# Strassen's scheme for the output product of a gated FFN, in groups of two pairs

## The chip, the cores and the metric

The kernel runs on one core of a Trainium2 chip. The metric is the device time of one execution in microseconds (us). TensorE is called PE, VectorE DVE, ScalarE ACT, GpSimd POOL; SP issues the DMAs. PEld is PE's loading of weights.

## The reference, cut to what matters

```python
x = attention(q, k, v)                     # 2304 tokens x 512, window of 128, sloped bias
x = gelu_like(x @ w_in) @ w_out            # first FFN, 512 -> 2048 -> 512
g = x @ w_gate                             # second FFN, 512 -> 1536, twice
silu = g * (1.0 / (1.0 + np.exp(-g)))
val = x @ w_val
return (silu * val @ w_out2).astype(np.float32)   # 1536 -> 512
```

Inputs come as float64 words for the weights; the result has to be close to float32.

## The kernel before, in words

**Precision.** PE's operands have the type fp32r, a float32 word of fewer fraction bits. To keep float32's accuracy every operand is split in two: a rounded upper part, written by ACT as a copy, and the rest, written by DVE as a difference. A product is three matmuls: upper by upper, upper by rest, rest by upper.

**Stages.** Attention is computed in blocks of tokens and lies between the matmuls of the first FFN, in an order that is written out by hand for its start (`PLAN`) and set by hooks after it. The first FFN leaves its result y, transposed, in a scratch tensor in HBM (`y_scratch`). The second FFN, about 517 to 935 us, works on three super-blocks of 768 tokens. Its hidden width of 1536 is taken in six *pairs* of two 128-wide chunks, so there are 18 pair steps, q = 0 to 17. The words "gate" and "value" (G, V) stand for the products with `w_gate` and `w_val`, "O" for that with `w_out2`.

**Gate and value by Strassen.** For a pair, G and V are each a 2 x 2 block product (halves of the 512 inputs with halves of the tokens, for two chunks), and are computed with the Winograd form of Strassen's scheme: seven products in place of eight, numbered 1 to 7 (`product`, L690). One product is six matmuls of 384 columns (two chunks of the contraction by three splits). Products 1, 6, 7, 4 accumulate in one PSUM bank, 2 in a second, 5 and 3 in a third (`gv_steps`, L704). ACT copies partial sums out (`keep_copy`), DVE adds them (`add`), and behind products 2, 3, 7 and 4 of V a quarter of the pair's hidden tile is finished (`gate`, L719): tanh on ACT, two DVE instructions, then the split into upper part (ACT) and rest (DVE, L729).

**The output product** is done directly (`o_part`, L757): for each of six 128-token tiles, six matmuls of 512 columns into one bank, and one DVE instruction that adds it to an accumulator of 128 x 512 in SBUF (ACT copies it for the first pair of a super-block). It runs one pair behind G and V; the program puts one tile into the next pair's products and five behind them. After the last pair of a super-block each accumulator is written to the result.

**Preparation.** The Strassen sums of the weights are made on the chip while the first FFN runs, and the rest early in the second: a unit is one half of one pair of one matrix (36 units: 6 pairs x G, V, O x 2). `fetch` (L238) loads it, `fraction` turns the 64-bit words into float32, four DVE sums (L271) make the combinations, `halves` splits them (ACT L229, DVE L230), and two DMAs store them in a scratch tensor. Units of O have no sums: one split of 512 columns. `advance` spreads these steps over the program by a rate per block (`PACE`, `PACE_LATE`). The combinations of y (seven pieces per super-block, `y_steps`, L638) are made on DVE and ACT, with seven splits and four differences of 768 columns.

**What sets the order.** Instructions are recorded in program order, and a scheduler then orders them on each engine by its own estimate; the queues run in that order. Each weight tile of the second FFN (`load_weights`, L675) has one buffer: its next load waits on SP until PE has done its last product.

```python
for pair in ((1, 5), (2, 6), (3,), (7,), (4,)):   # gv_steps
    for m in "GV":
        for i in pair:
            step(m, i)
            yield m, i
```

Of the kernel before, what the change touches and what calls it, by code (L numbers as in the profile page):

```python
# [26 lines left out]
PACE = {0: 1.4, 2: 2.0, 3: 2.2, 4: 2.3}  # L27

PAUSE = 77

PACE_LATE = 0.6
# [3 lines left out]
LATER = 2.5  # L35

SUPER = 6

O_ORDER = 3, 4, 5, 0, 1, 2

A_BLOCKS = (4, 2, 4, 4, 4)
# [40 lines left out]
def attention_two_ffn(ctx: ExitStack, tc: tile.TileContext, q, k, v, w_in, w_out, w_gate, w_val, w_out2, yscr, wscr, woscr, out):  # L82
# [9 lines left out]
    DM = out.shape[1]  # L92
# [25 lines left out]
    wpool = ctx.enter_context(tc.tile_pool(name="w", bufs=1, reuse_waits="tile"))  # L118
    cvp = ctx.enter_context(tc.tile_pool(name="cv", bufs=2))
# [107 lines left out]

    def halves(t, at, src):
        nc.scalar.activation(out=t[:, at, 0, :], in_=src, func=AF.Copy)  # L229
        nc.vector.tensor_tensor(out=t[:, at, 1, :], in0=src, in1=t[:, at, 0, :].bitcast(F32), op=ALU.subtract)  # L230
# [3 lines left out]

    def fetch(slot, unit):

        m, p, h = unit
        pool, tag = slot()  # L238
        if m == "O":
            raw = pool.tile([P, 512, 2], U32, tag=tag, name="raw")  # L240
            src = w_out2[(2 * p + h) * P : (2 * p + h + 1) * P, :].bitcast(U32)
            nc.sync.dma_start(out=raw.rearrange("p c w -> p (c w)"), in_=src)
            return raw
        raw = pool.tile([P, 2, 2, P, 2], U32, tag=tag, name="raw")
        w = w_gate if m == "G" else w_val
        for f in range(2):
            src = w[2 * p + f].bitcast(U32).rearrange("p (a b c) -> p a b c", a=2, b=2)[:, :, h, :]
            nc.sync.dma_start(out=raw[:, f].rearrange("p a c w -> p a (c w)"), in_=src)
        return raw.rearrange("p f a c w -> p (f a c) w")

    def prepare(slot, raw, fetch_next, unit):

        m, p, h = unit
        cs = cvp.tile([P, 8, P], F32, tag="cv", name="cs")
        yield from fraction(raw, cs)
        fetch_next()
        if m == "O":
            pool, tag = slot()
# [16 lines left out]
        at = wscr[p, "GV".index(m)]  # L275
        pool, tag = slot()
        wa = pool.tile([P, 4, 2, P], F32R, tag=tag, name="wa")
# [5 lines left out]
        wb = cvp.tile([P, 3, 2, P], F32R, tag="cv", name="wb")  # L283
# [317 lines left out]
    def y_part(j, f):  # L601
# [36 lines left out]
    def y_steps(s, tile_of):  # L638
# [3 lines left out]
        def quarter(i, j):  # L642
            t = yrp.tile([P, 2, HT], F32, tag="yr", name="yr")
# [31 lines left out]
    def load_weights(q, m, half):  # L675
        p = q % NP2
        if m == "O":
            t = wpool.tile([P, 2, 2, 512], F32R, tag="w11" if q < NS * NP2 - 1 else "w0", name="wo")
            nc.sync.dma_start(out=t.bitcast(F32).rearrange("p f r c -> p (f r c)"), in_=woscr[p])
        else:  # L680
            n = (4, 3)[half]
            t = wpool.tile([P, 2, n, 2, P], F32R, tag=f"w{7 + 2 * 'GV'.index(m) + half}", name="wg")
            at = wscr[p, "GV".index(m)]
            nc.sync.dma_start(
                out=t.bitcast(F32).rearrange("p h s r c -> p (h s r c)"),
                in_=at[:, :2048] if half == 0 else at[:, 2048:],
            )
        w2[q, m, half] = t

    def product(q, m, i, bank_, start):  # L690
        half, at = W_OF[i]
        w, y = w2[q, m, half], y2[q // NP2, i]
        for kk in range(2):
            for n, (a, b) in enumerate(((0, 0), (0, 1), (1, 0))):
# [3 lines left out]
                    rhs=y[:, b, kk, :],  # L698
# [5 lines left out]
    def gv_steps(q):  # L704

        banks, kept, c = {}, {}, {}
        p2[q] = [wpool.tile([P, 2, 2 * HT], F32R, tag=f"w{12 + 2 * (q % 2) + f}", name="p2") for f in range(2)]
# [10 lines left out]

        def gate(i):  # L719
            f, j = i  # L720
            g, v = c["G", i], c["V", i]
            at = slice(j * HT, (j + 1) * HT)
            th = pp.tile([P, HT], F32, tag="th2", name="th2", bufs=3)
# [340 lines left out]
```

## Time and profile before

| what | value |
|---|---|
| median of three runs | 938.6 us (938.53 to 939.38) |
| profiled execution | 937.2 us, of which the span from first to last instruction is 935.4 |
| PE busy, share of the span | 916.7 us, 98% |
| DVE, ACT, POOL busy | 649.0, 422.0, 123.6 us |
| granted TensorE clock, mean | 0.994 |
| HBM read and written | 142.6 and 38.8 MB |

The busy time of an engine is the time in which at least one of its instructions runs. The chain that ended last is followed back from the last instruction; where its pieces follow each other without a gap, the engine named in them sets the time.

### The profile page before, as it was taken

How to read it: one execution, taken by the hardware profiler on the slowest of the kernel's cores; microseconds unless marked ns; L12 is line 12 of the kernel's file. 1: busy time of each engine (PE TensorE's matmuls, PEld its weight loads, DVE VectorE, ACT ScalarE, POOL GpSimd, SP SyncE). 2: the span in 40 equal slices, each digit the busy share in tenths (PEclk: the TensorE clock that was granted, in tenths of full speed). 3: DMA queues.
4: the chain of work that ended last, by engine and by line, in shares of the span. 5: the costliest groups of instructions: out<-in, count | busy, mean ns of one | idle time of the engine just before them, and what ended most of it. 6: DMA issues, size and time to landing. Idle time of an engine off the chain costs nothing.

```text
span 935.4 us, 15014 instructions
## 1 busy us (share of the span) xinstructions
PE 916.7 (98%) x5464; PEld 788.6 (84%) x5464; DVE 649.0 (69%) x1558; ACT 422.0 (45%) x968; POOL 123.6 (13%) x221
## 2 busy tenths in 40 slices
PE   6899999999999999999999999999999999999998
PEld 4577898787778877788888999999999999999996
DVE  7898797756876668757696567577545577545555
ACT  5565565643654446534454453344343343342321
POOL 4744004512331023300000000000000000000000
PEclk9899999999999999999999999999999999999999
DMA  8953202425543355435579488667765666766641
GB/s 319 358 200 134 93 13 62 151 93 166 176 150 128 126 195 192 139 108 191 196 267 325 166 333 322 226 211 265 265 209 203 208 255 220 275 213 216 212 151 67
DMA packets 62473, 182.38 MB, mean 195 GB/s; under 512 B 6080, under 2 KB 28096, under 8 KB 55488
## 3 DMA queue, kind: packets, MB, share of 16 engines
q1 hardware_dynamic: 62400, 181.43, 55.1%
q8 instruction: 43, 0.70, 0.3%
q14 instruction: 30, 0.25, 0.1%
HBM read 142.61 MB, written 38.80 MB: 194 GB/s over the span
## 4 chain that ended last, share of the span: by engine, by line
PE 86%; DVE 6%; DMA 3%; ACT 2%; POOL 1%; issue 1%; SPq 0%; DVEq 0%; POOLq 0%; ACTq 0%
PE sx L695 16%; PE o L765 16%; PE sz L695 8%; PE hp L561 6%; PE y L561 6%; PE hp L563 6%; PE y L563 6%; PE hp L562 6%; PE y L562 6%; PE sy L695 4%; PE xb L514 2%; PE sb L361 2%; PE pt L453 1%; DMA y_scratch<-yt 1%; DVE wraw L194 1%; POOL prob L421 1%
## 5 line engine op out<-in xcount | busy, mean ns | idle before, releaser
L695 PE MATMUL sx<-ya,wg 128*128 128x384 f32 x864 | 172.6, 336 | 0.0
L765 PE MATMUL o<-wo,p 128*128 128x512 f32 x648 | 158.9, 391 | 0.0
L695 PEld LDWEIGHTS sx<-ya,wg 128*128 128x128 f32 x864 | 153.1, 188 | 5.5 <-issue 0.3
L765 PEld LDWEIGHTS o<-wo,p 128*128 128x128 f32 x648 | 120.8, 188 | 21.4
L561 PE MATMUL hp<-xh,wt 128*128 128x512 f32 (+1 forms) x320 | 121.0, 378 | 0.5 <-DVE th L584 0.4
L563 PE MATMUL hp<-xh,wt 128*128 128x512 f32 (+1 forms) x320 | 118.1, 370 | 0.0
L562 PE MATMUL hp<-xl,wt 128*128 128x512 f32 (+1 forms) x320 | 118.0, 369 | 0.0
L562 PE MATMUL y<-gl,wt 128*128 128x512 f32 (+1 forms) x320 | 116.8, 371 | 0.5 <-DVE gl L592 0.5
L563 PE MATMUL y<-gh,wt 128*128 128x512 f32 (+1 forms) x320 | 117.0, 371 | 0.0
L561 PE MATMUL y<-gh,wt 128*128 128x512 f32 (+1 forms) x320 | 111.2, 377 | 0.2 <-DVE stat L386 0.2
L421 POOL TENSOR_SCALAR prob<-prob,stat 128x128 f32<-128x128 f32 x144 | 68.9, 498 | 204.4 <-DVE sb L331 55.7
L695 PE MATMUL sz<-ya,wg 128*128 128x384 f32 x432 | 84.1, 335 | 0.0
L592 DVE TENSOR_TENSOR gl<-th,gh 128x512 fp32r<-128x512 f32 (+1 forms) x80 | 52.4, 659 | 44.7 <-ACT gh L590 44.3
L590 ACT ACTIVATE gh<-th 128x512 fp32r<-128x512 f32 (+1 forms) x80 | 46.7, 586 | 78.5 <-PE y L563 55.2
L774 DVE SCALAR_TENSOR_TENSOR acc<-o,acc 128x512 f32<-128x512 f32 x90 | 61.4, 688 | 25.1 <-PE o L765 23.9
L695 PEld LDWEIGHTS sz<-ya,wg 128*128 128x128 f32 x432 | 75.8, 188 | 0.2
L716 DVE TENSOR_TENSOR c<-sy,pc 128x384 f32<-128x384 f32 x36 | 20.1, 558 | 79.5 <-PE sy L695 75.3
L561 PEld LDWEIGHTS hp<-xh,wt 128*128 128x128 f32 x320 | 60.4, 189 | 13.6 <-issue 1.6
L402 ACT ACTIVATE prob<-prob,stat 128x128 f32<-128x128 f32 x144 | 56.2, 392 | 34.4 <-DVE stat L386 34.3
L563 PEld LDWEIGHTS y<-gh,wt 128*128 128x128 f32 x320 | 60.3, 188 | 11.2 <-issue 1.0
L562 PEld LDWEIGHTS y<-gl,wt 128*128 128x128 f32 x320 | 60.3, 189 | 10.9 <-DVE gl L592 0.9
L563 PEld LDWEIGHTS hp<-xh,wt 128*128 128x128 f32 x320 | 60.2, 188 | 10.6
(90 smaller groups left out, 1385.6 us busy)
## 6 DMA issues: line engine op xcount, KB each, us to landing
wg<-w_scratch SPq DMA_DIRECT2D x36, 1024.0 KB, 6.9
wg<-w_scratch SPq DMA_DIRECT2D x36, 768.0 KB, 5.2
wo<-wo_scratch SPq DMA_DIRECT2D x18, 1024.0 KB, 6.9
w_scratch<-wa SPq DMA_DIRECT2D x24, 512.0 KB, 2.7
w_scratch<-wb SPq DMA_DIRECT2D x24, 384.0 KB, 3.5
wraw<-in_moe_w_in SPq DMA_DIRECT2D x16, 512.0 KB, 6.7
wraw<-in_moe_w_out SPq DMA_DIRECT2D x16, 512.0 KB, 7.3
raw<-in_moe_w_gate SPq DMA_DIRECT2D x24, 256.0 KB, 3.3
```

What stands on the lines that cost most here:

```text
L361: nc.tensor.matmul(out=sb[e][c : c + size, (i % 2) * 256 + lo : (i % 2) * 256 + hi], lhsT=u["q"][rows, i * P + c : i * P + c + size], rhs= ...
L402: nc.scalar.activation(out=prob[:, x], in_=prob[:, x], func=AF.Exp, bias=stat[:, 0, x : x + 1], scale=-1.0, accum_out=stat[:, 1, x : x + 1],)
L421: (nc.vector if (j, hp, g) in NORM_ON_VECTOR else nc.gpsimd).tensor_scalar(out=prob[:, x], in0=prob[:, x], scalar1=stat[:, 3, x : x + 1], ...
L561: nc.tensor.matmul(out=out_ap, lhsT=whi, rhs=xhi, start=start, stop=False)
L562: nc.tensor.matmul(out=out_ap, lhsT=whi, rhs=xlo, start=False, stop=False)
L563: nc.tensor.matmul(out=out_ap, lhsT=wlo, rhs=xhi, start=False, stop=stop)
L590: a = nc.scalar.activation(out=gh[:, :m], in_=th[:, :m], func=AF.Copy)
L592: d = nc.vector.tensor_tensor(out=gl[:, :m], in0=th[:, :m], in1=gh[:, :m].bitcast(F32), op=ALU.subtract)
L695: nc.tensor.matmul(out=bank_[:, :HT], lhsT=w[:, kk, at, a, :], rhs=y[:, b, kk, :], start=start and kk == 0 and n == 0, stop=kk == 1 and n ...
L716: marks["d"] = nc.vector.tensor_tensor(out=t, in0=b[:, :HT], in1=kept[m, k], op=ALU.add).ins
L765: nc.tensor.matmul(out=o, lhsT=ph[:, a, c], rhs=w[:, f, b, :], start=f == 0 and n == 0, stop=f == 1 and n == 2)
L774: nc.vector.scalar_tensor_tensor(out=acc, in0=o, scalar=0.5, in1=acc, op0=ALU.mult, op1=ALU.add)
```

## The change

The output product is computed by the same seven-product scheme as G and V, transposed: two pairs form a group (a contraction of 512), the 512 outputs are halved twice, and the tokens are halved once. A group has two half-groups of seven products; `o_steps(q)` is one of them and lies between the products of pair q, two pairs behind. The result is written transposed, and the host turns it back.

- Hidden quarters are no longer split alone. `pieces_of` forms the seven token-side combinations of a pair with four differences on DVE, and splits them; the splits of pieces 2 and 3 go to POOL (`ON_POOL`), five stay on DVE, the upper parts are ACT's.
- Each output product that ends a bank's content is added to one of eight 128 x 384 accumulators by DVE; in a super-block's first group products 1, 5, 6 and 4 are copied by ACT.
- The O units get sums and splits like the others. More units are prepared in the first FFN (`PACE`), and five are left for the second, from pair 2 on; the last differences of these five are POOL's (`late`).
- The differences of y for super-blocks 1 and 2 go to POOL, the seven pieces of y have one set of buffers, and are made in the last pair of the super-block before.
- G and V take product 7 ahead of 3. `w_out2`'s weights are loaded as 1024 and 768 KB per half-group, with one buffer each.

```diff
-PACE = {0: 1.4, 2: 2.0, 3: 2.2, 4: 2.3}
-PAUSE = 77
-PACE_LATE = 0.6
-LATER = 2.5
-O_ORDER = 3, 4, 5, 0, 1, 2
+PACE = {0: 2.0, 2: 2.4, 3: 2.5, 4: 2.7}
+REST = 74
+LATE, PACE_LATE = 2, 0.8
+P_BUFS = 24
+ON_POOL = 2, 3
+O_STEPS = 1, 5, 6, 2, 7, 3, 4
...
     def halves(t, at, src):
         nc.scalar.activation(out=t[:, at, 0, :], in_=src, func=AF.Copy)
-        nc.vector.tensor_tensor(out=t[:, at, 1, :], in0=src, in1=t[:, at, 0, :].bitcast(F32), op=ALU.subtract)
+        engine = nc.vector if late[0] is None else nc.gpsimd
+        engine.tensor_tensor(out=t[:, at, 1, :], in0=src, in1=t[:, at, 0, :].bitcast(F32), op=ALU.subtract)
...
-        if m == "O":
-            pool, tag = slot()
-            t = pool.tile([P, 1, 2, 512], F32R, tag=tag, name="wo")
-            halves(t, slice(0, 1), cs.rearrange("p s c -> p (s c)")[:, :512].unsqueeze(1))
-            nc.sync.dma_start(out=woscr[p][:, h * 1024 : (h + 1) * 1024], in_=flat(t))
-            yield
-            return
...
         def minus(out_, a, b):
-            nc.vector.tensor_tensor(out=out_, in0=a, in1=b, op=ALU.subtract)
+            (nc.gpsimd if s else nc.vector).tensor_tensor(out=out_, in0=a, in1=b, op=ALU.subtract)
...
+                    rhs=p2[2 * (q // 2 - 1) + kk, i][:, b, :] if m == "O" else y2[q // NP2, i][:, b, kk, :],
...
+        def split(i, src):
+            t = pp.tile([P, 2, HT], F32R, tag="p", name="p2", bufs=P_BUFS)
+            nc.scalar.activation(out=t[:, 0], in_=src, func=AF.Copy)
+            engine = nc.gpsimd if i in ON_POOL else nc.vector
+            engine.tensor_tensor(out=t[:, 1], in0=src, in1=t[:, 0].bitcast(F32), op=ALU.subtract)
+            p2[q, i] = t
...
-            ph = p2[q][f]
-            nc.scalar.activation(out=ph[:, 0, at], in_=th, func=AF.Copy)
-            nc.vector.tensor_tensor(out=ph[:, 1, at], in0=th, in1=ph[:, 0, at].bitcast(F32), op=ALU.subtract)
+            b[i] = th
+        def pieces_of(i):
+            gate(i)
+            if i == (0, 0):
+                split(1, b[i])
+            elif i == (1, 1):
+                split(3, b[i])
+            elif i == (0, 1):
+                b11, b12, b22 = b[0, 0], b[i], b[1, 1]
+                minus(b11, b12, b11)
+                split(5, b11)
+                minus(b12, b22, b12)
+                split(7, b12)
+                minus(b22, b22, b11)
+                split(6, b22)
+            else:
+                split(2, b[i])
+                minus(b[i], b[i], b[1, 1])
+                split(4, b[i])
...
-        for pair in ((1, 5), (2, 6), (3,), (7,), (4,)):
+        for pair in ((1, 5), (2, 6), (7,), (3,), (4,)):
...
-    def o_part(q, i):
...
+    def o_steps(q):
+        banks = {}
+        g, half = q // 2 - 1, q % 2
+        s, first, last = g // 3, g % 3 == 0, g % 3 == 2
+        for i in O_STEPS:
+            x = {1: "x", 6: "x", 7: "x", 4: "x", 2: "y", 5: "z", 3: "z"}[i]
...
+            product(q, "O", i, t, new)
+            a, b = {1: (0, 0), 2: (0, 0), 6: (0, 1), 3: (0, 1), 5: (1, 1), 7: (1, 1), 4: (1, 0)}[i]
+            if first and i in (1, 5, 6, 4):
+                acc = pp.tile([P, HT], F32, tag=f"acc{half}{a}{b}", name="acc")
+                o2[half, a, b] = acc
+                nc.scalar.activation(out=acc, in_=t[:, :HT], func=AF.Copy, scale=0.5)
+            else:
+                acc = o2[half, a, b]
+                nc.vector.scalar_tensor_tensor(out=acc, in0=t[:, :HT], scalar=0.5, in1=acc, op0=ALU.mult, op1=ALU.add)
+            if last and i in (2, 3, 7, 4):
+                rows, cols = (2 * a + half) * P, s * SUPER * P + b * HT
+                nc.sync.dma_start(out=out[rows : rows + P, cols : cols + HT], in_=acc)
+            yield i
...
+        if s + 1 < NS and p == NP2 - 1:
+            pieces[s + 1] = y_steps(s + 1, piece, slot)
+        behind = o_steps(q) if q > 1 else iter(())
         for n, (m, i) in enumerate(gv_steps(q)):
-            if q or n > 5:
+            if q >= LATE:
                 advance(PACE_LATE)
...
+            if n % 2:
+                done = next(behind, None)
+                if done and q < NQ - 1:
+                    last_weights(q, done)
...
+    for _ in zip(o_steps(NQ), o_steps(NQ + 1)):
+        pass
```

Three places show how the instructions are moved. First PE, in a pair without other work. Before (pair 4, from its products 3 on; `sx`, `sy`, `sz` are banks of G and V, `o` that of the output, `p` the split hidden tiles):

```order
L695 MATMUL sz<-ya,wg 128x384 x12
L695 MATMUL sx<-ya,wg 128x384 x6
L765 MATMUL o<-wo,p_6214 128x512 x3
L765 MATMUL o<-wo,p_6215 128x512 x2
L695 MATMUL sx<-ya,wg 128x384 x6
L765 MATMUL o<-wo,p_6215 128x512
L765 MATMUL o<-wo,p_6214 128x512 x3
L765 MATMUL o<-wo,p_6215 128x512 x3
```

And now (pair 8, from product 1 of V on; `ox`, `oy`, `oz` are banks of the output product):

```order
L715 MATMUL sx<-ya,wg 128x384 x6
L715 MATMUL sz<-ya,wg 128x384 x6
L715 MATMUL oz<-p_7219,wg 128x384 x3
L715 MATMUL oz<-p_7442,wg 128x384 x3
L715 MATMUL sy<-ya,wg 128x384 x6
L715 MATMUL sx<-ya,wg 128x384 x6
L715 MATMUL ox<-p_7227,wg 128x384 x3
L715 MATMUL ox<-p_7450,wg 128x384 x3
L715 MATMUL sy<-ya,wg 128x384 x6
L715 MATMUL sx<-ya,wg 128x384 x6
L715 MATMUL oy<-p_7256,wg 128x384 x3
L715 MATMUL oy<-p_7479,wg 128x384 x3
```

Output matmuls of 512 columns that stood mostly behind the pair's products have become products of 384 columns that stand one behind every two of them.

Second DVE, behind product 3 or 7 of V, where a pair's last quarters are finished. Before (pair 9, with `c2` the sums of partial products, `th2` the hidden quarters, `acc` the accumulators):

```order
L716 TENSOR_TENSOR c2_7571<-sx_7473,pc_7489 128x384 [waits PE_49]
L774 SCALAR_TENSOR_TENSOR acc_7184<-o_7579,acc_7184 128x512 [waits PE_49]
L726 TENSOR_TENSOR th2_7573<-th2_7573,c2_7571 128x384 [waits DVE_49]
L774 SCALAR_TENSOR_TENSOR acc_7215<-o_7609,acc_7215 128x512 [waits PE_49]
L729 TENSOR_TENSOR p2_7454<-th2_7573,p2_7454 128x384 [waits Activation_49]
L774 SCALAR_TENSOR_TENSOR acc_7224<-o_7617,acc_7224 128x512 [waits PE_49]
L725 SCALAR_TENSOR_TENSOR th2_7601<-th2_7601,sx_7455 128x384 [waits Activation_49]
```

And now (pair 6):

```order
L752 SCALAR_TENSOR_TENSOR th2_7252<-th2_7252,sx_7052 128x384 [waits Activation_49]
L739 TENSOR_TENSOR th2_7139<-th2_7214,th2_7139 128x384 [waits DVE_49]
L753 TENSOR_TENSOR th2_7252<-th2_7252,sx_7078 128x384 [waits DVE_49,PE_49]
L739 TENSOR_TENSOR th2_7214<-th2_7183,th2_7214 128x384 [waits DVE_49]
L745 TENSOR_TENSOR p2_7219<-th2_7139,p2_7219 128x384 [waits Activation_49]
L739 TENSOR_TENSOR th2_7183<-th2_7183,th2_7139 128x384 [waits DVE_49,Pool_49]
L822 SCALAR_TENSOR_TENSOR acc_6273<-ox_7070,acc_6273 128x384 [waits PE_49]
L745 TENSOR_TENSOR p2_7223<-th2_7214,p2_7223 128x384 [waits Activation_49]
L745 TENSOR_TENSOR p2_7227<-th2_7183,p2_7227 128x384 [waits Activation_49]
L739 TENSOR_TENSOR th2_7252<-th2_7252,th2_7183 128x384 [waits Pool_49]
L822 SCALAR_TENSOR_TENSOR acc_6308<-ox_7293,acc_6308 128x384 [waits PE_49]
L745 TENSOR_TENSOR p2_7260<-th2_7252,p2_7260 128x384 [waits Activation_49]
```

Differences and splits of the pieces stand together behind the gate of the last quarters, some of them wait for POOL, and the accumulations of the next output products stand among and behind them.

Third POOL, which has nothing in the second FFN before. Now, in pairs 4 and 5 (with `wa`, `wb` the split weights of a late unit, `yr` the pieces of y):

```order
L239 TENSOR_TENSOR wa_6704<-cs_6601,wa_6704 128x2x128 [waits DMAHW3_49,Activation_49]
L239 TENSOR_TENSOR wb_6747<-cs_6601,wb_6747 128x3x128 [waits DMAHW5_49,DMAHW6_49,DMAHW1_49,Activation_49]
L745 TENSOR_TENSOR p2_6684<-th2_6680,p2_6684 128x384 [waits PE_49,Activation_49]
L745 TENSOR_TENSOR p2_6763<-th2_6759,p2_6763 128x384 [waits DVE_49,Activation_49]
L658 TENSOR_TENSOR yr_6821<-yr_6823,yr_6821 128x768 [waits DMAHW6_49,DMAHW1_49,DMAHW7_49,DVE_49,Pool_49]
L658 TENSOR_TENSOR yr_6823<-yr_6825,yr_6823 128x768 [waits DMAHW2_49,DMAHW0_49,Pool_49]
L658 TENSOR_TENSOR yr_6821<-yr_6825,yr_6821 128x768 [waits DVE_49]
L745 TENSOR_TENSOR p2_6960<-th2_6956,p2_6960 128x384 [waits PE_49,Activation_49]
```

Splits of the hidden pieces, of the late weights and the differences of y have come into one in-order queue.

## Rows read from the trace of the kernel before

**Rows 1.** page, part 1: busy us (share), instructions

```profile
PE 916.7 (98%) x5464; PEld 788.6 (84%) x5464; DVE 649.0 (69%) x1558; ACT 422.0 (45%) x968; POOL 123.6 (13%) x221
```

**Rows 2.** windows: us, busy PE, PEld, DVE, ACT, POOL, clock, DMA share, GB/s

```profile
517.60:931.60 414.00, 413.90 (x2172) 386.13 (x2171) 258.17 (x463) 151.88 (x299) 0.00 (x0) 1.00 0.64 226
160.00:517.50 357.50, 357.17 (x2299) 285.11 (x2290) 254.77 (x718) 175.95 (x437) 65.99 (x125) 1.00 0.49 171
```

**Rows 3.** chain, second FFN: start us, us, engine, tile, line

```profile
535.17 4.16 PE sx L695 x24
...
657.38 2.08 PE sz L695 x12
...
680.33 2.08 PE sz L695 x12
...
886.12 2.08 PE sz L695 x12
...
908.91 2.08 PE sz L695 x12
...
920.19 11.36 PE o L765 x50
...
931.57 0.69 DVE acc L774
```

**Rows 4.** groups by line: count | busy us, mean ns | idle before

```profile
L765 PE MATMUL o<-wo,p 128*128 128x512 f32 x648 | 158.9, 391 | 0.0
...
L695 PEld LDWEIGHTS sx<-ya,wg 128*128 128x128 f32 x864 | 153.1, 188 | 5.5 <-issue 0.3
```

**Rows 5.** groups of DVE, window of the second FFN (517.6 to 931.6)

```profile
L774 DVE SCALAR_TENSOR_TENSOR acc<-o,acc 128x512 f32<-128x512 f32 x90 | 61.4, 688 | 25.1 <-PE o L765 23.9
...
L729 DVE TENSOR_TENSOR p<-th,p 128x384 fp32r<-128x384 f32 x72 | 39.9, 554 | 15.4 <-ACT p L728 15.4
...
L725 DVE SCALAR_TENSOR_TENSOR th<-th,c 128x384 f32<-128x384 f32 x54 | 30.1, 557 | 10.6 <-ACT th L724 8.9
...
L716 DVE TENSOR_TENSOR c<-sx,pc 128x384 f32<-128x384 f32 x36 | 20.0, 556 | 0.5
...
L651 DVE TENSOR_TENSOR ya<-yr,ya 128x768 fp32r<-128x768 f32 x14 | 13.3, 950 | 0.0
...
L655 DVE TENSOR_TENSOR yr<-yr 128x768 f32<-128x768 f32 x8 | 7.6, 952 | 0.0
```

**Rows 6.** single lines: count, ns min/median/max, first and last start

```profile
L271 DVE TENSOR_TENSOR cs<-cs x96: 275/284/721, 172.0 to 500.9; 128x128 f32<-128x128 f32 x96
...
L729 DVE TENSOR_TENSOR p<-th,p x72: 548/552/561, 529.1 to 921.4; 128x384 fp32r<-128x384 f32 x72
...
L421 POOL TENSOR_SCALAR prob<-prob,stat x144: 365/375/2388, 11.7 to 396.2; 128x128 f32<-128x128 f32 x144
...
L478 POOL TENSOR_SCALAR_AFFINE_SELECT pf<-pf x34: 632/638/1687, 15.8 to 405.9; 128x512 f32<-128x512 f32 x34
```

**Rows 7.** groups by line, the multiplication on POOL

```profile
L421 POOL TENSOR_SCALAR prob<-prob,stat 128x128 f32<-128x128 f32 x144 | 68.9, 498 | 204.4 <-DVE sb L331 55.7 <-ACT gh L590 51.9 <-DVE stat L415 45.6
```

**Rows 8.** groups by line, weight preparation on DVE

```profile
L271 DVE TENSOR_TENSOR cs<-cs 128x128 f32<-128x128 f32 x96 | 26.2, 302 | 0.8
...
L230 DVE TENSOR_TENSOR wa<-cs,wa 128x256 fp32r<-128x256 f32 x48 | 19.4, 431 | 0.8 <-ACT wa L229 0.8
...
L230 DVE TENSOR_TENSOR wb<-cs,wb 128x384 fp32r<-128x384 f32 x24 | 13.5, 561 | 0.3 <-ACT wb L229 0.3
...
L230 DVE TENSOR_TENSOR wo<-cs,wo 128x512 fp32r<-128x512 f32 x12 | 8.2, 685 | 0.5 <-ACT wo L229 0.3
...
L223 DVE SCALAR_TENSOR_TENSOR cs<-cs,raw 128x512 uint32<-128x512 uint32 x36 | 25.7, 713 | 0.5
```

**Rows 9.** window of 540 to 560; DMA issues: KB each, us to landing

```profile
540.00:560.00 20.00, 20.00 (x106) 18.55 (x105) 13.86 (x27) 12.18 (x24) 0.00 (x0) 1.00 0.89 338
...
wg<-w_scratch SPq DMA_DIRECT2D x36, 1024.0 KB, 6.9
```

More of the change, by code (lines that the diff above doesn't have):

```diff
@@ L675, in load_weights @@
     def load_weights(q, m, half):
[L676 removed]
+        n, k = (4, 3)[half], "GVO".index(m)
         if m == "O":
[L678 to L687 removed]
+            g = (q // 2 - 1) % (NP2 // 2)
+            prepared(*((m, 2 * g + kk, q % 2) for kk in range(2)))
+        else:
+            prepared(*((m, q % NP2, h) for h in range(2)))
+        at_end = m == "O" and q > NS * NP2
+        pool, tag = (pp, f"wo{half}") if m == "O" and not at_end else (kept, f"w{KEPT[k % 2 * 2 + half]}")
+        t = pool.tile([P, 2, n, 2, P], F32R, tag=tag, name="wg")
+        at = woscr[(q // 2 - 1) % (NP2 // 2), q % 2] if m == "O" else wscr[q % NP2, k]
+        nc.sync.dma_start(
+            out=t.bitcast(F32).rearrange("p h s r c -> p (h s r c)"),
+            in_=at[:, :2048] if half == 0 else at[:, 2048:],
+        )
         w2[q, m, half] = t
@@ L917, in attention_two_ffn, with slot, fetch_next, prepared @@
     bctx = ExitStack()
-    todo = [(m, p, h) for p in range(NP2) for m in "GVO" for h in range(2)]
-    todo.sort(key=lambda u: u[1] + (LATER if u[0] == "O" else 0))
-    closed, turn = [], [0]
-    def slot():
-        if not closed:
-            return att, "er"
-        turn[0] += 1
-        return wpool, f"w{(turn[0] - 1) % O_SLOTS}"
-    def preparation():
-        raws = []
-        def fetch_next():
-            if len(raws) < len(todo):
-                raws.append(fetch(slot, todo[len(raws)]))
-        fetch_next()
-        yield
-        for i, u in enumerate(todo):
-            yield from prepare(slot, raws[i], fetch_next, u)
+    todo = [(m, p, h) for m in "GVO" for p in range(NP2) for h in range(2)]
+    todo.sort(key=lambda u: u[1] if u[0] != "O" else 4.5 if u[1] < 4 else 6)
+    where, turn, rest = [att], [0], [False]
+    def slot(shape, dtype, name):
+        pool, tag = where[0], "er"
+        if pool is att and name in ("cs", "wb"):
+            pool, tag = cvp, "cv"
+        elif pool is wpool:
+            turn[0] += 1
+            tag = f"w{7 + (turn[0] - 1) % O_SLOTS}"
+        return pool.tile(shape, dtype, tag=tag, name=name, bufs=2 if pool in (att, cvp) else 1 if pool is wpool else 4)
+    ready, busy = {}, [False]
+    def preparation():
+        for i, u in enumerate(todo):
+            def fetch_next(i=i + 1):
+                if i < len(todo) and not rest[0]:
+                    ready[i] = fetch(slot, todo[i])
+            while i not in ready:
+                fetch_next(i)
+                yield
+            busy[0] = True
+            yield from prepare(slot, ready.pop(i), fetch_next, u)
+            busy[0] = False
+            made.add(u)
+    def prepared(*wanted):
+        while not made.issuperset(wanted):
+            in_order(work)
+    made = set()
     work, owed = preparation(), [0.0]
@@ L952, in advance, with settle @@
             in_order(work)
+    def settle(pool):
+        rest[0] = True
+        while busy[0] or ready:
+            in_order(work)
+        rest[0] = False
+        where[0] = pool
     for idx, (j, f) in enumerate(seq):
```

180 lines of the change are left out of this document (89 added, 91 removed).

## The prediction

> **What bounds the kernel now.** I read the page's first part, then the two stretches, then the chain, then the groups of DVE and POOL. The first part shows TensorE (PE) busy 916.7 of 935.4 us [rows 1]. A busy share alone proves little, because matmuls overlap; the window of the second FFN says more: from 517.6 to 931.6 us PE is busy 413.9 of 414.0 us, DVE 258.2, POOL not at all [rows 2]. The chain there consists of PE pieces that follow each other with no gap [rows 3]. So the second FFN lasts as long as its matmuls take to be issued, and a matmul that falls away is time that falls away, as long as DVE, ACT and the weight loads keep up.
>
> The chain also gives the price of a matmul. 24 products' matmuls of 384 columns take 4.16 us, which is 0.1733 us each, and the same point of pair 16 and of pair 17 lies at 886.12 and 908.91 us, 22.79 us apart. A pair issues 84 matmuls of 384 columns for gate and value (14.56 us) and 36 of 512 columns for the output; the rest, 8.23 us, gives 0.2285 us each. The 50 at the end agree (11.36 us, 0.2272 each). In six pairs around 650 to 780 us the distance is 22.95, at the same full granted clock; I carry that 1 us of the whole stage over unchanged.
>
> **The sum on PE.** The 648 output matmuls of 512 columns [rows 4] go: 648 x 0.2285 = 148.1 us. In their place come 18 half-groups of 7 products with 6 matmuls of 384 columns, 756 x 0.1733 = 131.0 us: the same shape as gate and value have, so I take their price. That is 17.1 us less; the stage goes from 414.0 to 396.9, a pair with output work from 22.79 to 126 x 0.1733 = 21.84 us. The last accumulation is 384 wide in place of 512 (0.56 for 0.69 us [rows 3, 5]): 0.1 less. Pairs 0 and 1 now have no output work to lie between their products; it comes in one piece of 84 matmuls (14.6 us) behind pair 17, which moves work and adds none. **Gain 17.2 us if nothing waits.**
>
> **DVE in the second FFN.** Per stage it loses 90 accumulations of 512 (61.4 us), 72 old splits (39.9) and the 8 differences of y, which go to POOL (7.6) [rows 5]. It gains 90 splits and 72 token differences at 0.554, and 102 accumulations at 0.557 (the other 24 are ACT's): 49.9 + 39.9 + 56.8 = 146.6. The late weight preparation is about even: six plain output units before, five Strassen units now whose last differences are POOL's. So 258.2 - 108.9 + 146.6 = 296 us of 397, 75% for 62%. ACT, busy 151.9 of 414 [rows 2], gets 54 more copies of about 0.5 us and stays under half.
>
> An average hides the dense pairs. Counting the DVE rows of the new order from one pair's first y-sum to the next, at row durations, pairs 2 to 6 ask for 19.7, 18.5, 21.7, 22.2 and 18.3 us (sum 100.4), pairs 11 and 12 for 20.7 and 18.3, the plain pairs for 14.4 to 16.6. PE needs 21.84 per pair, 109.2 for the five. Pair 5's count is 27 instructions of 0.556, seven splits of y at 0.95, and two 128-column sums. So pairs 4 and 5 are full and the others have slack. Before, the fullest pairs asked for 19.8 of 22.79, and PE never waited. Pairs 0 and 1 ask for 12.7 and 13.3 of 14.56.
>
> The in-order queue matters in a plain pair too. The burst behind product 3 of the value matrix, most of it in the order shown, is some 13 instructions, 7.2 us. Meanwhile PE issues O3, G4, O4, V4, and of the next pair G1, G5, O1, V1, V5, O5, G2: 11.5 us. What PE needs first from DVE behind it is the accumulation of the next O1, whose bank O6 overwrites, about 12.5 us after the burst began. 3 to 5 us of lateness are free.
>
> **POOL.** It gets 36 splits of 384 columns, 15 late weight splits and 8 differences of 768. No row shows a POOL instruction with two inputs. Below stands the one-input select, 0.638 us for 512 columns, so 0.48 for 384; above, the longest POOL row, 2.39 us [rows 6]. I take twice the select's rate, 0.96 us, since two operands are read where it reads one; that sum is 61 us in all, 28.5 of it in pairs 2 to 6 and 11.5 in pairs 11 and 12. POOL's own time hides beside everything.
>
> What it does to DVE is the question. With POOL silent, DVE's split lasts 548/552/561 ns. In the attention stretches, where POOL works, DVE's small sums have a median of 284 ns and reach 721, and POOL's multiplication has a median of 375 and reaches 2388 [rows 6]: they hold each other up. But mostly it is POOL that pays: its 144 multiplications have a mean of 498, so 144 x 0.123 = 17.7 us lost [rows 7], and the 96 sums of DVE lost 96 x (0.302 - 0.284) = 1.7 [rows 6, 8]. Let f be the part of POOL's time that DVE loses. DVE is late in the dense pairs by (100.4 + 28.5 f - 109.2) + (39.0 + 11.5 f - 43.7) = 40 f - 13.5 us, which is nothing below f = 0.34. The few rows say well under 0.2. Still, pairs 4 and 5 are full by themselves, pair 1 nearly, and an in-order queue never fills perfectly: I charge **2 us**, between 0 (before, no wait) and 6.
>
> The Trainium skill, page "SBUF — State Buffer", section "Who interferes with whom", says that a DVE instruction with two SBUF inputs contends with a GpSimd instruction that reads SBUF, and that the loser blocks until the other is done. The stretched rows agree with it; if DVE were always the loser, f would be 1, and that is the slower rival below.
>
> **First FFN.** 31 weight units are prepared there for 30, and all by Strassen. By the order that is 28 more sums (0.302), 14 more pair splits (0.431), 7 more triple splits (0.561), 6 plain ones (0.685) fewer, and one unit's three bit operations (at most 0.713 each) [rows 8]: 8.5 + 6.0 + 3.9 - 4.1 + 2.1 = 16.4 us of DVE. DVE is busy 254.8 of 357.5 us there while PE is busy 357.2 [rows 2], so its 102.7 us of spare time hide it: 0, at most 1 if a piece falls into a burst.
>
> **Weight loads.** A pair loads 5.25 MB for 4.5. Every tile has one buffer and is refilled once PE has left it; the shortest time to the next use is O2 to the next O1, 12 products or 12.5 us, against 6.9 us for 1024 KB [rows 9]. In the dense pairs preparation and y come on top: 5.5 MB + 1.8 MB per 21.84 us is 334 GB/s, just what the trace shows at 540 to 560 us (338, with PE at 20.00 of 20.00). No charge, but no room either.
>
> **Sum.** The profiled execution took 937.2 us: 937.2 - 17.2 + 2 = 922.0. It lies 1.4 below the median of the three runs, 938.6 (lowest 938.53); against the median, **923.4 us**.
>
> **Rivals.**
> - *POOL holds DVE one for one* (f = 1): the dense pairs run 26.5 us late, and 938.6 - 17.2 + 26.5 = 947.9, slower. It is slower from 40 f - 13.5 > 17.2, f above 0.77. For it: 721 ns for a 284 ns sum. Against: the sums lost 1.7 us where the multiplications lost 17.7. Chance 0.08.
> - *The dense pairs stall half as badly* (f near 0.5: 6.5 us), or a weight load lands late there at the transfer rate limit, about 1 us in each of five pairs (5 us): 926 to 930. For it: counts of 21.7 and 22.2 us against 21.84, and 334 GB/s against 338. Chance 0.16.
> - *The change does not shorten PE*: it has 108 more weight loads, and one lasts 188 ns [rows 4]. Were a product held to that, 756 x 0.188 = 142.1 would save 5.9, and the time be 934.6. Against: gate and value matmuls already run at 0.1733 with the same loads. Chance 0.03.
> - *Queue losses in nearly every pair* (1 us x 16) undo the gain: 937.4 to 939. Chance 0.03.
> - Forecast, 920.5 to 926: chance 0.70.
>
> 0.2% of 938.6 is 1.9 us, about what a measurement of this kernel can tell from no change. Slower is the first rival, same is most of the fourth, the rest is faster: 0.90, 0.02, 0.08. The lower end is the full gain less half a us of noise and rate, 920.5; the upper takes in the forecast and most of the second rival, 930.5, with 0.82 between.
>
> **What the new profile would show.** Right: about 2268 matmuls of 384 columns in the second FFN at 0.173 us, pairs of 21.8 us, a stage of 397 to 400; any wait of PE is on DVE in pairs 4 to 6. POOL's splits near 1 us and stretched, DVE's split median still about 0.55. Wrong: PE gaps in the plain pairs (8, 9, 14 to 16), DVE splits well over 0.6 us in the median, weight loads landing after 12 us, or a first FFN longer than 517.6 us.

## The result, and the profile after

| what | before | after |
|---|---|---|
| median, four runs each | 939.0 us (938.53 to 939.65) | 928.3 us (927.28 to 932.85) |
| profiled execution; its span | 937.2; 935.4 us | 928.64; 926.9 us |
| second FFN, start of its first product to end of its last (PE's rows) | 517.43 to 931.53: 414.1 us | 521.51 to 923.34: 401.8 us |

The ratio is 0.9895, 95% interval 0.9862 to 0.9929: faster, by 10.7 us, where 15.2 were forecast and 920.5 to 930.5 was the range. Five later executions of the same kernel, further down, took 926.65 to 930.23; the median of all nine is 928.6.

The profiled execution was forecast at 922.0 and took 928.64. Where the 6.6 us lie is read in the same order as before. First the page's first part, the answer to [rows 1]: DVE has 60 us more, GpSimd 70, PE 14 less.

```profile
PE 902.6 (97%) x5572; PEld 799.8 (86%) x5572; DVE 708.9 (76%) x1709; ACT 452.9 (49%) x1052; POOL 193.5 (21%) x280
```

Then the windows, as in [rows 2] (us, busy PE, PEld, DVE, ACT, POOL, clock, DMA share, GB/s). The second FFN now holds 3.1 us in which PE is idle, where it had 0.1; DVE is busy 305 of 402 us (I had counted 296).

```profile
521.67:923.40 401.73, 398.62 (x2281) 396.06 (x2279) 305.36 (x574) 176.02 (x369) 72.36 (x59) 1.00 0.78 280
```

The chain, as in [rows 3] (start us, us, engine, tile, line), has the same point of a pair at these places. Plain pairs are 21.92 us apart (815.67, 837.59), 126 matmuls at 0.174 us; I had forecast 21.84 and 0.1733. From 616.22 to 706.08 four pairs took 89.86, which is 2.2 more than four times 21.92.

```profile
616.22 1.21 PE sz L715 x7
...
706.08 1.21 PE sz L715 x7
...
815.67 1.21 PE sz L715 x7
...
837.59 1.21 PE sz L715 x7
```

PE's timeline shows where it stood (start us, us, engine, line, tiles, count, and in brackets its idle time and what ended it). The 24 matmuls begun at 534.69 are issued by 538.87; the next product, pair 1's first, starts at 540.62, held by a weight load. The other two gaps are in pairs 6 and 7 (536 and 600 matmuls of gate and value are issued before them, at 84 a pair), just behind the pairs that I had counted as the fullest, and behind ACT, which waited for DVE.

```profile
534.69 4.33 PE L715 MATMUL sx<-ya,wg 128*128 128x384 f32 x24
540.62 1.31 PE L715 MATMUL sx<-ya,wg 128*128 128x384 f32 x6 [1.60 <-DMA wg<-w_scratch]
...
651.45 0.45 PE L715 MATMUL oz<-p,wg 128*128 128x384 f32 x1 [0.77 <-ACT p L743]
...
669.41 1.31 PE L715 MATMUL sx<-ya,wg 128*128 128x384 f32 x6 [0.56 <-ACT pc L730]
```

The chain ahead of the last of them (start us, us, engine, tile, line):

```profile
667.96 0.48 DVE th L739
668.46 0.53 ACT p L743
668.98 0.39 ACT pc L730
```

SP's timeline suggests why pair 1's load was late (`r6` below tests it): `load_weights` for pair 2's output products, 1.75 MB that PE first reads at 556.7, is issued at 527.78, 4 us ahead of pair 1's own weights.

```profile
527.78 1.20 SPq L704 DMA_DIRECT2D wg<-wo_scratch  x2
529.07 1.37 SPq L260 DMA_DIRECT2D raw<-in_moe_w_val  x2
531.76 7.60 SPq L704 DMA_DIRECT2D wg<-w_scratch  x4
```

The largest piece lies ahead of all this: the second FFN starts 4.1 us later. To tell the start-up from the first FFN I took one matmul of the first FFN's hidden products (line 565, before 562), the 101st and the last of its 320, in each trace:

| run | 101st, us | last, us | growth over the kernel before |
|---|---|---|---|
| before; its second execution | 162.21; 162.11 | 511.54; 511.93 | 0; +0.5 |
| after; its second and third | 163.66; 162.61; 163.36 | 515.62; 515.08; 515.85 | +2.6; +3.1; +3.2 |

So some 3 us are lost in the first FFN each time; in the five further runs whose first FFN is unedited (`r3`, `r4`, `r6`, `r7`, `r10`) the growth is 2.3 to 3.5. The other 1.45 us of the first trace, ahead of the 101st product, vary between executions: in the second of the same kernel they are 0.4. From 45 to 60 us the mean granted clock was 0.89 in the first, 1.00 in the second, 0.95 in the kernel before. The windows of after and of its second execution:

```profile
45.00:60.00 15.00, 12.51 (x70) 9.11 (x67) 14.24 (x34) 9.51 (x20) 8.44 (x10) 0.89 0.68 248
```

```profile
45.00:60.00 15.00, 13.83 (x90) 10.07 (x87) 14.24 (x34) 9.92 (x21) 8.44 (x10) 1.00 0.75 279
```

PE's waits in the first FFN of after (160 to 517 us: us in total, times, longest) all end on DVE, 2.1 us; before there were 0.4. The rest of the growth, some 0.9 us, is in no wait that the profile names.

```profile
PE y L564 <- DVE yt L628: 0.9, 1, 0.9
PE xb L517 <- DVE stat L389: 0.7, 1, 0.7
PE y L564 <- DVE stat L389: 0.5, 1, 0.5
```

Ahead of the two waits on `stat` (175.8 and 249.8 us) DVE worked without a pause for 2 us or more, with pieces of the weight preparation between those of attention. The wait on `yt`, the longest, is of another kind: DVE itself had been idle for 0.83 us, for a load from `y_scratch`. The chain there (as above):

```profile
218.51 0.48 SPq L288
...
219.03 4.06 DMA part<-y_scratch
...
224.31 3.18 DMA part<-y_scratch
...
227.58 0.70 DVE yt L628
...
228.33 0.50 PE y L564
```

L288 stores prepared weights. That store waited for DVE, the first load of `part` was issued right behind it, and the second behind the `yt` that the first had held up. So a part of this wait is the place of transfers in SP's queue.

### The profile page after: what moved, and what is told of

Its sections match the earlier page's. It is cut to its first block, busy times and chain, and to the rows that moved or that the text cites. A ratio compares the mean times of both kernels' runs of the same rounds, so it can differ in the third digit from the quotient of the medians.

```text
span 926.9 us, 15758 instructions
## 1 busy us (share of the span) xinstructions
PE 902.6 (97%) x5572; PEld 799.8 (86%) x5572; DVE 708.9 (76%) x1709; ACT 452.9 (49%) x1052; POOL 193.5 (21%) x280
## 4 chain that ended last, share of the span: by engine, by line
PE 80%; DVE 10%; DMA 3%; ACT 3%; POOL 2%; issue 1%; SPq 1%; DVEq 0%; ACTq 0%; POOLq 0%
PE sx L715 14%; PE ox L715 7%; PE sz L715 7%; PE y L564 6%; PE hp L564 6%; PE y L566 6%; PE y L565 6%; PE hp L566 6%; PE hp L565 6%; PE sy L715 4%; PE oz L715 4%; PE xb L517 2%; PE oy L715 2%; PE sb L364 2%; PE pt L456 1%; POOL prob L424 1%
## 5 line engine op out<-in xcount | busy, mean ns | idle before, releaser
L745 POOL TENSOR_TENSOR p<-th,p 128x384 fp32r<-128x384 f32 x36 | 41.4, 1151 | 386.9 <-ACT p L743 381.8
L715 PE MATMUL ox<-p,wg 128*128 128x384 f32 x432 | 90.3, 337 | 0.0
L715 PE MATMUL sz<-ya,wg 128*128 128x384 f32 x432 | 88.2, 336 | 0.0
L743 ACT ACTIVATE p<-th 128x384 fp32r<-128x384 f32 x126 | 63.9, 521 | 46.4 <-DVE th L739 36.7
L715 PEld LDWEIGHTS ox<-p,wg 128*128 128x128 f32 x432 | 76.5, 188 | 0.4 <-ACT p L743 0.3
L745 DVE TENSOR_TENSOR p<-th,p 128x384 fp32r<-128x384 f32 x90 | 52.5, 589 | 24.1 <-ACT p L743 23.2
L564 PEld LDWEIGHTS y<-gh,wt 128*128 128x128 f32 x320 | 57.3, 188 | 14.8 <-issue 2.6
```

Of the source, the lines that this page charges most:

```text
L564: nc.tensor.matmul(out=out_ap, lhsT=whi, rhs=xhi, start=start, stop=False)
L715: nc.tensor.matmul(out=bank_[:, :HT], lhsT=w[:, kk, at, a, :], rhs=p2[2 * (q // 2 - 1) + kk, i][:, b, :] if m == "O" else y2[q // NP2, i][ ...
L743: nc.scalar.activation(out=t[:, 0], in_=src, func=AF.Copy)
L745: engine.tensor_tensor(out=t[:, 1], in0=src, in1=t[:, 0].bitcast(F32), op=ALU.subtract)
```

## The experiments

My theories: the missing time is lost (1) in the first FFN, to its denser DVE, (2) before pair 1, to the order of the weight loads on SP, (3) in the dense pairs, to DVE and to what GpSimd does to it. Rivals: variation between executions, a full DMA, or DVE's count alone.

**Controls.** The two kernels unedited (`r1`, `r2`, and `r5` beside later runs).

> The kernel before once more, unedited, as a control of one look. If the time lost ahead of the second FFN belongs to the program: the first product of the second FFN at 517.6 us again (within 0.3), the clock full from the first product of the first FFN on, as in its first profile. If it is variation between executions: anywhere between 516 and 521 us.

> The changed kernel once more, unedited. Program theory: the first product of the second FFN at 521.7 us again (within 0.3), low clock for some 3 us around 51 us again, PE idle 1.6 us on a weight load near 539 us and 1.3 us between 650 and 670 us. Variation theory: the 1.4 us lost to the low clock around 51 us are gone, and the second FFN starts near 520.

> The changed kernel unedited, timed beside the three that follow. Median 928.2, between 927.3 and 928.7; the second FFN lasts 401.8 us from its first product to its last in both profiles so far, so 401.8 again (within 0.2), with the gap of 1.7 to 1.8 us before pair 1 and about 1.9 us between 649 and 670.

Measured: 937.71, 928.09 and 930.0 us (926.65 to 930.23). The first product of the second FFN starts at 517.82, 520.97 and 521.74; the stage lasts 414.2, 401.83 and 403.2. `r5` missed what I expected, its median by 1.3 us and its stage by 1.4. The clock of 45 to 60 us was 1.00 in `r2` and 0.93 in `r5`. The growth of 3 us in the first FFN came in both, and so did the gap before pair 1 (1.81, 1.74). The dense pairs vary: in `r5` a third gap of 1.14 us joined the two, on a load of output weights at 672 us. So less than half of the 4.1 us is variation.

**Pair 1's loads.** First the output loads behind all four of pair 1's:

```diff
-                load_weights(2, "O", n // 13)
+                with tc.issue_after(last_of_1[0]):     # pair 1's last weight load
+                    load_weights(2, "O", n // 13)
```

> Only the two loads of the first output weights (1.75 MB, for pair 2) are moved on SP's queue, from ahead of pair 1's four weight loads to behind them. Theory A (pair 1's gate weights land late because 1.75 MB of output weights that nobody needs before 556 us were issued ahead of them): the first load of pair 1 lands in 6 to 7 us instead of 9, the gap of 1.75 us before pair 1 goes, the second FFN is 1.8 to 2.1 us shorter, time 926.3. Rival B (DVE and ACT are behind there anyway, the load only ended last): the gap stays within 0.5 us with another releaser, time 928. Rival C: the gap moves to the first output product near 556 us, time 928.

Measured: 929.55 us (928.19 to 930.51), stage 404.2. The first load landed in 6.5 us, as theory A had it, but the scheduler, working by its own estimate, had put pair 1's first product two products earlier, so PE still waited 1.45 us, at 537.44; and pair 2's first weights, now behind 1.75 MB, landed 1.67 us late, at 556.00. A miss, and a gap like C's, on other weights. The second try fixes both: one output load goes behind pair 1's second load, one behind its fourth, and pair 1's first product behind pair 0's last on PE.

```diff
+                with tc.issue_after(behind[n // 13]):  # pair 1's load V 0, then V 1
+                    load_weights(2, "O", n // 13)
...
+            with tc.issue_after(ends[0, "V", 4].ins) if (q, m, i) == (1, "G", 1) else ExitStack():
+                product(q, m, i, t, new)
```

> The two loads of pair 2's output weights go behind the first two and the last of pair 1's four weight loads, and PE keeps pair 1's first product behind pair 0's last (the run with the loads behind all four moved both). Theory A (the loads' order on SP makes pair 1's first weights late): they land 6.5 to 7 us after issue, 537.5, when PE wants them at 538.3; the gap before pair 1 goes, none comes before pair 2; the second FFN lasts 400.0, the time is 1.8 below the reference run. Rival G (the DMA engines are full there in any order): a gap of 1 us or more stays before pair 1 or pair 2, the time within 0.7 of the reference run.

Measured: **925.21 us** (925.05 to 926.68; ratio 0.9865, 0.985 to 0.9879); stage 399.5, 2.4 below the 401.8 of after. `r5`, timed beside it, had 930.0, so the median is 4.8 lower where I had expected 1.8; 2.0 us of it are the gaps before and in pair 1, and the rest lies ahead of the stage and in the dense pairs, which vary (3.6 us late in `r5`, 1.7 here). PE's timeline of this run has no gap where after had one (30 matmuls in one row, the next at 538.67 = 533.47 + 30 x 0.173), and SP's has the output loads apart:

```profile
533.47 5.36 PE L717 MATMUL sx<-ya,wg 128*128 128x384 f32 x30
538.67 1.21 PE L717 MATMUL sz<-ya,wg 128*128 128x384 f32 x6
```

```profile
530.54 2.40 SPq L704 DMA_DIRECT2D wg<-w_scratch  x2
533.00 0.42 SPq L704 DMA_DIRECT2D wg<-wo_scratch  x1
536.78 1.36 SPq L704 DMA_DIRECT2D wg<-w_scratch  x2
538.19 0.48 SPq L704 DMA_DIRECT2D wg<-wo_scratch  x1
```

Pair 1's two 1024 KB loads landed in 5.0 and 6.9 us for 8.8 and 9.2. Theory A holds: the same bytes, in another order, left no gap before pair 1 or pair 2.

**GpSimd silent.** `ON_POOL = ()`, the late splits and the differences of y on DVE.

> Everything that the change gave to GpSimd in the second FFN (36 splits, 15 late weight splits, 8 differences of y) is put back on DVE; GpSimd is silent there. Theory A (GpSimd holds DVE for 0.30 of its own time, so the loan pays): DVE loses 21.6 us of stretch and gets 34.7 us of work, in pairs 2 to 6 about 16.5 of work for 11 of stretch, and the dense pairs are 5 to 7 us late instead of 2.2: 931 to 933. Rival D (the dense pairs are late because of the stretching and of waits for GpSimd's queue, and DVE alone would do): no gap there, 926.

Measured: 926.67 us (926.6 to 927.07; ratio 0.9867, 0.9851 to 0.9883, for 0.9895 of after, whose interval overlaps), stage 401.5. Theory A fell: DVE was not 5 to 7 us late. The time is near D's 926, but gaps remained, on weight loads (0.68 us at 667.57, 1.11 at 669.97), none on DVE or ACT. The groups of DVE (busy us, mean ns | idle before, second FFN) show how little the loan is worth. In after:

```profile
L745 DVE TENSOR_TENSOR p<-th,p 128x384 fp32r<-128x384 f32 x90 | 52.5, 589 | 24.1 <-ACT p L743 23.2
L739 DVE TENSOR_TENSOR th<-th,th 128x384 f32<-128x384 f32 x72 | 44.0, 612 | 9.7 <-POOL p L745 9.4
L753 DVE TENSOR_TENSOR th<-th,c 128x384 f32<-128x384 f32 x54 | 34.7, 643 | 0.5
L752 DVE SCALAR_TENSOR_TENSOR th<-th,c 128x384 f32<-128x384 f32 x54 | 33.1, 615 | 10.5 <-ACT th L751 10.0
L735 DVE TENSOR_TENSOR c<-sx,pc 128x384 f32<-128x384 f32 x36 | 19.9, 554 | 12.9 <-PE sx L715 12.3
L654 DVE TENSOR_TENSOR ya<-yr,ya 128x768 fp32r<-128x768 f32 x14 | 17.6, 1262 | 0.0
...
L745 POOL TENSOR_TENSOR p<-th,p 128x384 fp32r<-128x384 f32 x36 | 41.4, 1151 | 386.9 <-ACT p L743 381.8 <-DVE acc L822 5.1
```

With GpSimd silent:

```profile
L745 DVE TENSOR_TENSOR p<-th,p 128x384 fp32r<-128x384 f32 x126 | 68.3, 553 | 23.6 <-ACT p L743 23.0
L739 DVE TENSOR_TENSOR th<-th,th 128x384 f32<-128x384 f32 x72 | 39.8, 553 | 0.5
L753 DVE TENSOR_TENSOR th<-th,c 128x384 f32<-128x384 f32 x54 | 29.9, 553 | 0.4
L752 DVE SCALAR_TENSOR_TENSOR th<-th,c 128x384 f32<-128x384 f32 x54 | 29.7, 552 | 6.3 <-ACT th L751 6.0
L735 DVE TENSOR_TENSOR c<-sx,pc 128x384 f32<-128x384 f32 x36 | 20.0, 556 | 13.7 <-PE sx L715 13.0
...
L654 DVE TENSOR_TENSOR ya<-yr,ya 128x768 fp32r<-128x768 f32 x14 | 13.2, 952 | 1.1 <-ACT ya L653 1.1
```

GpSimd works 72.4 us and DVE is busy 305.4 instead of 314.5: 9 us saved, and against them stand 9.4 us in which DVE waits for GpSimd's splits. In these rows only instructions with both inputs in SBUF are stretched: 612, 643, 615, 589 and 1262 ns for 553, 553, 552, 553 and 952; the sum with a bank among its inputs (L735) keeps 554. How it happens is in the timeline of after at 634 us: a split that starts while GpSimd works takes 1.84 us and ends at 636.51, 0.42 us behind the first of GpSimd's two instructions (636.09).

```profile
634.24 3.98 POOL L658 TENSOR_TENSOR yr<-yr 128x768 f32<-128x768 f32 x2 [7.42 <-DMA wg<-w_scratch]
634.66 1.84 DVE L745 TENSOR_TENSOR p<-th,p 128x384 fp32r<-128x384 f32 x1
...
637.57 1.07 DVE L752 SCALAR_TENSOR_TENSOR th<-th,c 128x384 f32<-128x384 f32 x1
```

The Trainium skill, page "SBUF — State Buffer", section "Who interferes with whom", says that a DVE instruction with two SBUF inputs contends with GpSimd's reads and that one with at most one, outside the modes that use two ports, does not; the trace agrees, with 612 for 553 ns on the one side and 554 for 556 (the mean of L735 with GpSimd silent) on the other.

**Output stores behind the weights**, so that none holds SP's queue.

> The output stores of a super-block go behind the next output weights on SP's queue, so that no weight load stands behind a store that waits for DVE. Theory E (SP, held by these stores for up to 3.6 us, issues the weight loads of pairs 6 and 7 too late): the gaps with a weight load as releaser between 660 and 672 go, 0.5 to 1.3 us; the time is 0.5 to 1 below the reference run. Rival (the gaps there are DVE's and ACT's lateness alone): no difference beyond 0.4.

Measured: 928.31 us (927.29 to 930.84), stage 402.2; the gaps at 650 and 668 us stay, on ACT (0.83 and 0.58). The stores held SP for 1.8 us between 640 and 680 us where they held it for 8.1 in after. The median lies 1.7 below that of `r5`, timed beside it, but the intervals of the two ratios overlap (0.988 to 0.9916, 0.9878 to 0.9922). No gap between 660 and 672 us ends on a weight load here; but there is none in the first trace of after either, 0.26 us in `r2` and, just behind that stretch, 1.14 in `r5`. So this run neither shows nor refutes theory E.

**The first FFN.** `PACE` of before (1.4, 2.0, 2.2, 2.3), and, apart from it, the four sums of the units prepared there left out (the combinations are then incomplete, and the run serves for timing alone).

> The rates of weight preparation in the first FFN are those of the kernel before (1.4, 2.0, 2.2, 2.3), so that about five units more are left for the second. Theory F (the first FFN is 3 us longer because of what is prepared in it): 5 units of 4.7 us DVE less, DVE's busy time there 245 instead of 268.6, below the 254.8 of before, and the second FFN begins near 517.6 to 518.5. It pays back: some 17 us of DVE and 7 MB more in pairs 2 to 5, which are full, so the second FFN is 5 to 15 us longer; time 930 to 940. Rival H (the first FFN is longer because its instructions stand in another order, whatever the amount): it begins at 520 to 521 again.

> In the first FFN the four sums of each of its 31 prepared weight units are left out (124 sums, 37 us of DVE; the combinations of weights are then wrong); loads, bit operations, splits and stores stay. Theory F1 (the first FFN is longer because DVE comes late to what attention and the FFN need): its extra time between 100 and 520 us, 2.6 to 3.3 us so far, falls below 1. Rival F2 (it is the transfers, or the order alone): it stays above 2. The second FFN as in the reference runs, 401.8 to 403.2.

Measured: 972.34 us (971.58 to 974.09) and 924.46. Windows of the stretch with attention in it, 160 to 420 us (columns as above), of after, of `r8` and of `r9`:

```profile
160.00:420.00 260.00, 257.90 (x1866) 202.60 (x1866) 198.94 (x622) 138.41 (x370) 67.08 (x128) 1.00 0.48 163
```

```profile
160.00:420.00 260.00, 259.17 (x1869) 203.72 (x1861) 184.54 (x587) 132.63 (x357) 66.62 (x125) 1.00 0.41 140
```

```profile
160.00:420.00 260.00, 260.00 (x1863) 205.18 (x1856) 180.11 (x540) 139.09 (x375) 63.93 (x124) 1.00 0.48 165
```

DVE's busy time there is 198.9, 184.5 and 180.1 us, and the growth of the first FFN +2.6, +0.8 and -0.9 (101st at 163.66, 162.40, 161.86; last at 515.62, 512.57, 510.26). `r9` moves as many bytes as after (165 for 163 GB/s) and has no idle PE. So the time goes with DVE's work and not with the number of bytes, as F1 had it. Which wait the work acts through is shown only in part: the scheduler also orders anew what is left (of DVE's other 762 instructions between 100 and 517 us 669 keep their order), and the wait on `yt`, which came through a late load, is gone too. Nor is the amount all: in `r8` DVE is as busy as before (184.5 for 185.3 us), and 0.8 us of growth is left. Preparing less there is no way out: in `r8` PE waits up to 23 us for output weights that are not made yet, and the stage lasts 450.3, 48.5 us more than after's where I had expected 5 to 15.

```profile
643.92 2.29 PE L715 MATMUL sx<-ya,wg 128*128 128x384 f32 x6 [9.81 <-DMA wg<-w_scratch]
...
693.42 1.97 PE L715 MATMUL ox<-p,wg 128*128 128x384 f32 x5 [23.18 <-DMA wg<-wo_scratch]
```

**Combinations.** Pair 1's order with GpSimd silent; the same with the preparation moved late (`PACE` 1.4, 2.0, 2.2, 4.0, `REST` 76); pair 1's order with GpSimd and a last rate of 5.0, `REST` 75.

> The run with pair 1's load order together with the run without GpSimd. Theory I (GpSimd's loan is worth nothing: the work it takes and the time for which it holds DVE cancel): the gaps on ACT and DVE between 647 and 668 us (1.4 us with GpSimd) go, the second FFN lasts 397.8 to 399, time 923.5 to 925, at most 1.5 below the run with pair 1's load order alone (925.2). Rival J (DVE's 13 us more of work, net, are late in the dense pairs): gaps on DVE of 2 us or more, 927 or above.

> The run before this one, with the same 31 units prepared in the first FFN, but fewer steps in its first three stretches (1.4, 2.0, 2.2, the rates of the kernel before) and more in its last (4.0, until its step 76), where attention is over. Theory F (early preparation in company of attention is what costs): the first FFN's extra time falls from 3.0 to 0.8 to 1.2 us, the second FFN is unchanged, time 921.5 to 923.5. Rival K (the faster rate only moves the lateness into the last stretch, before the second FFN's first product): no gain, 924 to 926.

> Pair 1's load order with GpSimd as in the change, and the preparation moved late in the first FFN as in the run before, at a rate of 5.0 there until step 75, which leaves four late units for the second FFN, not five. Theory F: the first FFN's extra time 0.8 to 1.2 us; the dense pairs lose less than 1.7 us with a unit less; time 922 to 924. Rival K: a first FFN that begins its last products late, 925 or more.

Measured: **925.27 us** (924.02 to 926.25; ratio 0.9851, 0.9837 to 0.9866), 941.4 (939.52 to 943.72) and 939.77 (938.22 to 941.81). `r10` equals `r6`: the gaps on ACT are gone, and loads land late instead, issued at 655.80 and 656.21, needed at 663.3 and 665.6, landed 8.6 and 10.7 us after issue. Theory I is right but for these 2.1 us (stage 400.0 for 397.8 to 399, time just above its 923.5 to 925); J falls:

```profile
664.54 1.28 PE L717 MATMUL sz<-ya,wg 128*128 128x384 f32 x6 [1.05 <-DMA wg<-w_scratch]
666.91 1.31 PE L717 MATMUL ox<-p,wg 128*128 128x384 f32 x6 [1.09 <-DMA wg<-wo_scratch]
```

In `r11` and `r12` the growth is +0.4 and +1.1 us, near the 0.8 to 1.2 of F, but they are no clean test of it: DVE did less ahead of the second FFN (254.6 and 257.9 us between 160 and 517.5 for 265.6 in after), because units slipped out of it. And 15 us are lost elsewhere, more than K said. The last units are not done when the first FFN ends, and ACT's copy of pair 0 stands behind them. PE's timeline and the chain of `r11`:

```profile
542.38 2.29 PE L717 MATMUL sx<-ya,wg 128*128 128x384 f32 x6 [15.05 <-ACT pc L732]
```

```profile
519.05 3.83 DMA raw<-in_moe_w_gate
...
526.66 3.80 DMA raw<-in_moe_w_gate
...
533.76 3.68 DMA raw<-in_moe_w_val
```

With one buffer for a unit's words, a unit is a chain of a 3.8 us load and 3.3 us of DVE and ACT: one per 7.1 to 7.6 us here, however high the rate that the program asks for.

## Why the prediction was right or wrong

The measured 928.3 us lies in the range of 920.5 to 930.5, but above the 920.5 to 926 that the forecast itself was given. It is where the second rival (dense pairs that stall half as badly, 926 to 930) would have put it, and not for that rival's reason: the dense pairs cost 2.2 us as charged. Two losses that I had put at nothing or nearly nothing, in the first FFN and before pair 1, and in the profiled execution a late start-up filled the place. That part of the hit is luck.

**The matmul sum was right.** 0.174 us a matmul for my 0.1733 and 21.92 us a pair for 21.84; 2268 x 0.174 + 2.7 us for the 12 matmuls of y among them is 397.4, against the 396.9 forecast.

**"It comes in one piece of 84 matmuls behind pair 17, which moves work and adds none"** failed: 2.0 us before and in pair 1 (1.75 and 0.27). The mistake is in my paragraph on weight loads. I took 12.5 us as the shortest time to a next use and compared rates; without output work between them, gate's first tile has 7.1 us from issue (531.76) to need (538.87), and the queue ahead of it held 1.75 MB for later. `r6` took the time back.

**"First FFN: 0, at most 1"** failed, and is the largest miss: 2.6 to 3.2 us. 102.7 us of spare DVE time is an average; the added work fell between what attention and the first FFN wait for (rows `stat`, `yt`). `r8` and `r9` show that the loss goes with DVE's work there. It is not DVE's time alone: the longest wait came through loads behind a store of prepared weights on SP, a way that my sum did not have at all. I had named a later start of the second FFN as the sign, and it came.

**The dense pairs, "2 us, between 0 and 6"**, were right in size: 2.2 us between the point of pair 4 and that of pair 8 in after and in `r2`, 3.6 in `r5`. The wait was the forecast one in after (DVE late, ACT behind it), though in pairs 6 and 7, where I had named 4 to 6. The reason was not: I charged it because DVE's count in pairs 4 and 5 was full by itself. With GpSimd silent (`r4`, `r10`) DVE has more to do and no gap of PE ends on DVE or ACT, so what made DVE late is most likely GpSimd's effect on it and the waits for GpSimd's splits, and not the count. That the size came out is luck to this extent. "No charge, but no room either" for the weight loads was close: near 670 us an output weight load ended a gap of 0.8 to 1.1 us in `r3`, `r4`, `r5`, `r9` and `r10` (0.3 in `r2`; in `r5` the load landed 12.8 us after issue, past my sign of 12), but none in after, `r6` or `r7`. This is the second half of the second rival, at one place where it had five.

**GpSimd's effect.** I took f well under 0.2. Stretched means against those of the silent run give 72 x 0.059 + 54 x 0.090 + 54 x 0.063 (L752) + 14 x 0.310 + 90 x 0.036 = 20 us of 72.4, f = 0.28. It stays under the 0.34 at which 40f - 13.5 turns positive, so the step's result held. The rival "one for one" fell. GpSimd's split took 1.15 us for my 0.96. The 20 us are part of the 305 us for which DVE was busy, so its work without them is some 285 us (an estimate from these rows): my count of 296, which held no stretch, came near by two errors that offset each other.

**The sum**, for the profiled execution: 922.0 forecast, + 1.45 start-up + 2.6 first FFN + 0.5 matmuls + 2.0 pair 1 + 0.2 dense pairs - 0.2 (the tail behind the last product, 3.6 for 3.9 us, of which 0.1 was forecast) = 928.55, measured 928.64.

## What to carry to other kernels

Spare time of an in-order engine over a whole stage hides nothing by itself: look at what stands between two instructions that the bounding engine waits for, there and now, on the DMA queue too. Where work is taken out between two uses of a single-buffered tile, count again from issue to need, with every transfer that the queue issues ahead of it, needed or not. Lending work to a second engine is worth its time only less what it holds up: here 72 us of GpSimd bought 9 us of DVE and no time (925.21 with it, 925.27 without).

## What was unexpected

GpSimd's 384-column split takes 1.01 us at its fastest, 1.8 times DVE's 0.553. The same program reached its 101st hidden product at 161.20 us (`r10`, unchanged up to there) to 163.66 (after). Of these 2.5 us 1.15 are there already at the first one (48.62 and 49.77). The two executions with the lowest granted clock from 45 to 60 us (0.89 in after, 0.93 in `r5`) are the two latest at the 101st, but at 1.00 it came at 161.20 to 162.61; no run here tried what decides that. Why the loads of `r10` land in 8.6 to 10.7 us around 656 us, at 348 GB/s over 640 to 668 us, was not taken apart either; in after such loads land in 7.7 to 11.1 us there, so it is not the lack of GpSimd alone.
